# A second-layer chain moved one step ahead, weights split in four and dummy matmuls in the opening

## The chip, the cores and the metric

The kernel runs on one core of one Trainium2 chip. The metric is the device time of one execution in microseconds (us), the median of several runs. The engines are named as in the profile: PE is TensorE (matmuls; PEld its weight loads), DVE VectorE, ACT ScalarE, POOL GpSimd, SP SyncE (which here only issues DMAs and DMA transposes).

## The reference

`x` has 2048 tokens of 512 numbers in bf16. Four blocks follow one another, two layers of A and then B:

```python
def A(x, mem, Wq, Wk, Wv, Wo):            # 32 heads of 128
    for s in range(64):                   # segments of 32 tokens
        h = concat([mem, x[32*s:32*s+32]])       # 8 memory rows + 32 tokens
        q, k, v = h @ Wq, h @ Wk, h @ Wv         # per head
        p = softmax(mask(q @ k.T / sqrt(128)))   # memory is seen by all, tokens causally
        o = (p @ v) @ Wo
        mem, out[s] = o[:8], o[8:]               # the next segment needs mem
def B(x, wqkv, wo):                       # linear attention, 32 heads of 16
    q, k, v = x @ wqkv
    pq, pk = phi(q), phi(k)               # phi(t) = (t+1 if t > 0 else exp(t)) + 1e-6
    kv, z = pk.T @ v, sum(pk)             # over all 2048 tokens
    return (pq @ kv) / (pq @ z + 1e-6) @ wo
x = x + A(LN(x)); x = x + B(LN(x)); x = x + A(LN(x)); x = x + B(LN(x))
```

A is a recurrence: segment s+1 can't be finished before the 8 memory rows that segment s produces. B needs the sums over all tokens (`kv`, `z`) before any token's output.

## The kernel before

**Steps and tiles.** A segment is a *step* s, 0 to 63 in each layer. Four steps make a *tile* of 128 tokens, and there are 16 tiles. Since the memory rows take 8 of 40 rows, a step's main block `hT` has 8 memory rows and the first 24 tokens of the segment; the last 8 tokens of the four segments of a tile are gathered in one block of 32 rows, the *left* block (`hTL`). Keys, queries and values of a left block are made once a tile, for four steps ahead (`left_block`, places left0, left1 and leftv); they must be there when the tile's first step begins.

**What one step does**, in the loop of `a_layer`: keys and queries of the main block (`project`, matmuls at L2154 and, with weights already loaded, L2042; `turned` evicts them at L1919 on ACT or L1920 on DVE and transposes them on DVE at L2173), values; for the 8 memory rows the scores, exponentials, sums and products with the values in two halves (`mem_attention`), the output projection (`out_proj`, L2408, then L2419 on DVE), and the product L2436 that picks the next memory rows out of it (`next_mem`). This is the chain from step to step. Beside it run the token rows of the same segment (`x_attention`), whose result joins the output projection a step later; the residual (`residual`, whose rows go by DMA from `y_sb` to `dx_sb`, issued on POOL at L1936 and on SP); and the B block's share. Everything that is not the chain is *fill* for TensorE.

**The B block inside the steps.** When a tile of A is complete, `b_in` normalises it, multiplies it by `wqkv` (`rows_of`, L2582), makes phi of keys in the buffer `e_sb` and of queries in `eq_sb`, adds to kv and z (L2653, L2660), and writes x to the scratch `xs` and phi(q) to the scratch `pq` in memory. Between the layers `b_mid` makes the block's final matrices. In the second layer, `tokens` calls `b_out` for each tile before its steps: it loads the x rows from `xs` (POOL, L1936), loads the transposed phi(q) rows from `pq` into `e_sb` by a DMA transpose on SP (L2082), multiplies by the summed z (`md`, 16 matmuls at L2054), takes the reciprocal, multiplies by kv and wo, and adds to x. Then `prepare` normalises the tile (places prep), turns it by another DMA transpose, and fills `hT` and the left block; then left0, left1 and leftv follow. So the second layer's chain from memory rows to the next tile's left keys and queries is: place bo, place prep, places left0 and left1. `e_sb` and the rooms for layer norm rows and reciprocals (`xlnT`, `vB`, `rB_sb`) are single buffers that `b_in` and `b_out` share. In the first layer, left blocks are fed straight from the input, and the left keys and queries of tiles 0 to 2 are made in the opening by `first_left_blocks` (places sk and sq).

**What sets the order.** Every instruction group is a *node*, recorded by `_Prog.add` under a place (layer, step, name) and a running count. Each node has a time in nanoseconds in the table `PLACE` (L16 to L1547), with a letter a or v where it may run on ACT or DVE. `schedule` sorts all nodes by these times; that is the whole order on each engine, and the letter chooses the engine. The times are a planner's due times, not measured ones; only their order enters the program. `schedule` also hands out the eight PSUM banks in that order, `finalize` places semaphore waits, and `emit` writes each engine's stream in order, so an instruction that waits holds up all that is behind it on its engine. `P.count += n` skips counts so that the table's entries stay with their nodes.

**The opening.** On SP's queue, one behind the other, stand the loads of Wk, Wq, Wv (4 MB each), 16 pieces of Wo (256 KB each) and wqkv (1.5 MB). ACT issues the memory rows and x of tile 0, POOL x of tiles 1 and 2 among some 50 instructions that make constants (place setup). TensorE transposes the x rows, multiplies by Wk as soon as it is there (sk, then the keys of step 0), then by Wq (sq, queries), then by Wv, and step 0 follows. A function `spin` for dummy matmuls is there, but nothing calls it.

Of the kernel before, what the change touches and what calls it, by code (L numbers as in the profile page):

```python
# [16 lines left out]
    (0, -9, 'setup'): '2751 2752 1621 15060 15061 16711 17238 20254 20902 21335 26596 31128 31613 36233 37053 37678 40093 41399 42472 43512 44808 60645 14865 0 560 1120 2190 2750 3310 17835 18402 18743 18744 18748 18959 18960 19391 20038 20470 21117 21333 21981 22197 22628 24910 25947 26595 27242 27673 27674 27675 27892 27891 29832 31127 32422 35143 39577a 17834 18745v 0 32839 35503 35506 36229 36234 29400 18746 0 0 0 0 0 0 0 0 0 0 0 0 0 0 0 0 0 0 0 0 0 0 0 0 0 0 0 0 0 0 0 0 0 0 0 0 0 0 0 0 0 0 0 0 0 0 0 0 0 0 0 0 0 0 0 0 0 0 0 0 0 0 0 0 0 0 0 0 0 0 0 0 0 0 0 0 0 0 0 0 0 0 0 0 0 27889 27890',  # L17
    (0, -4, 'start'): '19607a',
    (0, -2, 'leftv'): '37698 39210 39672 40371 41400a 41831 42471 42962a 44807 44810',
    (0, -2, 'prep'): '14142 14864 15059 15391 15647 16712 18006v 18749a 19393a 20471v 17833v',  # L20
    (0, -2, 'prepl'): '13340 14063 16713 18747 22198 22843 25550a',
    (0, 0, 'kq0'): '19821 20469 20901 22411 29615 29831 31126 31611 22843a 35502 32197v 34321',
    (0, 0, 'kq1'): '20685 22627 23714 26377 27672 28320 30046 30262 28751a 36228 34684v 32840a 35139',
    (0, 0, 'lq'): '730981 734917 735345 736139 737902 739038 739581 745577',
    (0, 0, 'lx'): '725135',
    (0, 0, 'mem0'): '36230 36232 37051 37314 37677 39560 40092 44809 43119 44811',
    (0, 0, 'mem1'): '36231 36726 37679 37681 42962 43400 43719 44806 45734 46451',
    (0, 0, 'next'): '48918 48972 49238v',
    (0, 0, 'out'): '45447 45515 46452 46605 46882 47101 47370 47588 48015a 48443',
    (0, 0, 'ql'): '35504a 34436a',  # L30
    (0, 0, 'sk'): '19390 21116 22196 23282 23707v 24430',
    (0, 0, 'sq'): '29183 29399 30910 31773 32197a 32838',
    (0, 0, 'v'): '39211 40967 41398 41830 42470a 44812a',
    (0, 0, 'x'): '38130 38346 38692 39560 39576 41401 40094 42262 48015 43282 43341 46451 48409 50344a 57004v 45446 46824 47807 48297 51423a 50345v',
    (0, 0, 'xl'): '1620',
    (0, 1, 'kq0'): '49480 49911 50343 50775 51855v 52419 51639a 52056',
    (0, 1, 'kq1'): '52419 52419 52501 52717 51206 51422 51638 51854 53141a 53782 52934a 52717a 52992',
    (0, 1, 'lq'): '756403 760618 760834 761049 762164 763460 764413 769975',
    (0, 1, 'mem0'): '52933 53423 53994 53795 54262 55249 55828 55830 55827 56230',
    (0, 1, 'mem1'): '53994 54876 55248 55829 55831 56230 56623 57442 56840 57443',  # L40
    (0, 1, 'next'): '59643 59697 59962a',
    (0, 1, 'out'): '56622 57003 57221 57440 58377 58378 58379 58717 58970a 59168',
    (0, 1, 'ql'): '40264a 39209v',
    (0, 1, 'res'): '65669 65917',
    (0, 1, 'sk'): '18958 20037 21332 21980 24908a 25549',
    (0, 1, 'sq'): '26161 26593 27456 28967 33316a 33958',
    (0, 1, 'v'): '52991 53523 54263 54444 55085v 56275a',
    (0, 1, 'x'): '55899 56274 57221 57444 57581 58716 58036 58376 59643 58718 58719 58969 59850 62803v 70329a 58851 58910 59168 59961 60644a 61939a',
    (0, 2, 'kq0'): '60212 60643 61075 61507 63018v 63151 62587a 63020',
    (0, 2, 'kq1'): '62802 63017 63290 63507 61938 62154 62370 62586 64587a 64588 63019a 63289a 63717',  # L50
    (0, 2, 'leftv'): '40535 42262 43511 44806 45446a 46088 47102 47371a 53348 57441',
    (0, 2, 'lq'): '762163 762379 763027 763243 764661 765609 767779 770110',
    (0, 2, 'lx'): '730981',
    (0, 2, 'mem0'): '63449 64586 65177 64958 65549 65916 66408 66717 66931 67239',
    (0, 2, 'mem1'): '64958 65176 65548 65668 65918 66158 66930 67238 67867 67868',
    (0, 2, 'next'): '70328 70382 70962v',
    (0, 2, 'out'): '67869 67870 67907 68125 68344 68562 68780 68999 69606a 69853',
    (0, 2, 'prep'): '15988 16710 16904 17237 17493 17968 18401v 26594v 20255a 24909v 29184a',
    (0, 2, 'ql'): '54469v 58910v',
    (0, 2, 'res'): '73922 79787',  # L60
    (0, 2, 'sk'): '19174 20253 21548 23498 27457a 27893',
    (0, 2, 'sq'): '28104 30478 30694 32421 35141a 35865',
    (0, 2, 'v'): '63723 64155 64959 65670 65916a 66933v',
    (0, 2, 'x'): '66408 66932 67451 67866 68781 69470 69130 68999 70496 69605 69853 69853 70753 75955a 81212v 69853 70436 70495 70641 70961a 71496v',
    (0, 3, 'kq0'): '71496 71537 72185 72616 73265a 73923 73921a 74831',
    (0, 3, 'kq1'): '73048 73696 74552 74559 70963 71969 73911 74127 75207a 75956 74551a 74830a 75955',
    (0, 3, 'lq'): '735345 757243 757954 760402 761049 762743 765002 785076',
    (0, 3, 'mem0'): '75206 75265 75836 75637 76342 77046 77047 77387 77180 77582',
    (0, 3, 'mem1'): '76343 76344 76658 77180 77045 77386 77975 78306 78192 78668',
    (0, 3, 'next'): '81044 81098 81364v',  # L70
    (0, 3, 'out'): '77974 78355 78573 78988 79060 79784 79785 79786 80399a 80569',
    (0, 3, 'ql'): '70193v 73911a',
    (0, 3, 'res'): '81365 89404',
    (0, 3, 'sk'): '18742 19606 21764 23066 27894a 28105',
    (0, 3, 'sq'): '31612 34437 35140 35142 37052v 37314',
    (0, 3, 'v'): '73264 74775 75837 75957 76659v 77388a',
    (0, 3, 'x'): '77386 77673 78027 78573 78987 79783 79442 79923 81098 80569 81211 81270 81364 85987a 86151a 80398 81152 81441 81499 86277v 86751v',
    (0, 4, 'kq0'): '81611 82043 82474 83122 83986v 84485 84485a 85065',
    (0, 4, 'kq1'): '82906 84486 84850 84851 83554 83769 83985 84485 85497a 85914 84904a 84849a 85332',
    (0, 4, 'lq'): '767175 767779 768593 774744 778783 779388 780112 785508',  # L80
    (0, 4, 'lx'): '754821',
    (0, 4, 'mem0'): '85496 85986 86358 87108 87110 87762 88094 88805 88311 88806',
    (0, 4, 'mem1'): '86518 86576 87327 87109 88311 88474 89023 89841 89022 90059',
    (0, 4, 'next'): '92261 92315 92581v',
    (0, 4, 'out'): '89403 89621 89840 90058 90276 90495 90713 90931 91358a 91786',
    (0, 4, 'ql'): '83987a 84848v',
    (0, 4, 'res'): '95415 97436 87107 87326 87544 87874 88092 88585 88804 89185 90495a 90713 92827 92824 95198 94120 92826 96826 94983 95199 97493',
    (0, 4, 'sk'): '25730 27241 27888 28536 30695v 30911',
    (0, 4, 'sq'): '32205 36835 37051 37680 38693v 38846',
    (0, 4, 'v'): '85064 85914 86151 86751 87763v 88093a',  # L90
    (0, 4, 'x'): '88585 91150 92825 92828 92829 94984 94119 94550 95414 96708 96825 97316 98357 99061a 100805v 96766 97375 97865 98804 102000a 104112a',
    (0, 4, 'xl'): '3810',
    (0, 5, 'kq0'): '92823 93254 93686 94118 95416a 96886 94982a 96885',
    (0, 5, 'kq1'): '94549 94765 94981 95197 95413 95628 95844 96060 96277a 97435 97434a 96484a 97866',
    (0, 5, 'lq'): '762595 763890 764412 765003 768386 771109 775937 776686',
    (0, 5, 'mem0'): '97433 97492 98359 97864 98708 100009 100144 100187 100143 100549',
    (0, 5, 'mem1'): '98277 98277 98911 98358 100008 101159 101478 101787 102002 102149',
    (0, 5, 'next'): '104710 104764 105030v',
    (0, 5, 'out'): '101014 101478 101489 102406 102543 102761 102979 103256 103683a 104111',
    (0, 5, 'ql'): '96827v 97437a',  # L100
    (0, 5, 'res'): '112945 107325',
    (0, 5, 'sk'): '25946 26809 27025 28751 30970a 31611',
    (0, 5, 'sq'): '32197 35505 37682 38130 39599a 40371',
    (0, 5, 'v'): '96276 96884 98360 99060 99400v 100550a',
    (0, 5, 'x'): '98468 99400 100008 100145 101012 101489 101607 102979 102405 102149 103198 103592 103710 110431a 105136v 103475 103534 103651 103822 105343v 105932a',
    (0, 6, 'bi'): '97867 98277 98471 98804 99060 101013 102001 104062 105031 111073 112515 114473 115695 118563 115731a 122891 139072 123323 141513 115356 115902 116404 124929',
    (0, 6, 'kq0'): '105465 106540 106544 107324 107832a 108473 107833v 108836',
# [1686 lines left out]
def _build_kernel(nc, A_x, A_mem0, A_Wq, A_Wk, A_Wv, A_Wo, A_seg_len, B_wqkv, B_wo, out):  # L1794
# [118 lines left out]
    P = _Prog(nc, banks)  # L1913
# [965 lines left out]
```

## Time and profile before

| | us |
|---|---|
| median of 3 runs (1577.38, 1580.69, 1579.38) | 1579.38 |
| the profiled execution | 1580.13 |
| its span (first to last instruction) | 1578.4 |
| mean granted TensorE clock | 0.997 |
| end of the opening: first product L2436 | 52.0 |
| first layer, steps 1 to 62 | 705.1 |
| joining of the layers (steps 63 and 0, `b_mid`) | 46 |
| second layer, steps 1 to 62 | 724.3 |
| tail behind them | 51 |

Landings in the opening, from issue to data: x of tile 1 at 8.6 us, of tile 0 at 10.1, of tile 2 at 10.2, Wk at 14.5, Wq at 25.7, Wv at 35.9, the last piece of Wo at 47.7, wqkv at 51.6.

How to read it: the page's busy shares say which engine has least idle time; the chain that ended last says what the end of the span hung on; the timeline lists single groups with start, length, engine, line, operation, tiles and what released them; the windows view gives, for a stretch, its length and then for PE, PEld, DVE, ACT and POOL the busy time with the number of instructions, then the granted clock, the DMA share and GB/s. Lines are those of the code above. The code counts the layers from 0; the text below calls its layer 0 "layer 1" and its layer 1 "layer 2".

### The profile page before, as it was taken

To read this page: it belongs to the slowest core of one execution; us is meant where nothing else is said; L and a number is where in the kernel's file an instruction comes from. 1 tells how busy PE (TensorE), PEld (TensorE's weight loads), DVE (VectorE), ACT (ScalarE), POOL (GpSimd) and SP (SyncE) were. 2 spreads that over 40 slices of the span, in tenths; PEclk is the share of its full clock that TensorE was granted. 3 is DMA by queue.
4 is the path that set the end of the run, shared out by engine and by line. 5 is a ranking of instruction groups with operands and counts; after the bars stand their busy time and mean duration, and the time that the engine had idled before them with its cause. 6 is when DMAs were issued, how large, how long until landed. Compare 5 with 4: busy or idle time off the path is not lost.

```text
span 1578.4 us, 97381 instructions
## 1 busy us (share of the span) xinstructions
PE 1511.5 (96%) x48481; PEld 822.8 (52%) x40705; DVE 1223.1 (77%) x3536; ACT 987.4 (63%) x3043; POOL 197.2 (12%) x396
## 2 busy tenths in 40 slices
PE   5899999999999999999999999999999999999997
PEld 2445555555555555555545555555555455555554
DVE  4577878887777788777878787888877787777778
ACT  2566665656666666665666666666576666576665
POOL 2011110111111011111111110111101011110110
PEclk9999999999999999999999999999999999999999
DMA  9301010110000000101310111111101111001124
GB/s 381 104 20 20 17 33 20 27 24 23 21 18 16 22 24 24 24 17 30 62 32 17 26 25 20 25 29 21 31 10 27 27 27 23 23 20 20 34 42 134
DMA packets 84819, 60.69 MB, mean 38 GB/s; under 512 B 64121, under 2 KB 78777, under 8 KB 82873
## 3 DMA queue, kind: packets, MB, share of 16 engines
q1 hardware_dynamic: 71096, 37.58, 9.7%
q0 software_dynamic: 13152, 16.75, 3.9%
q8 instruction: 349, 5.72, 1.5%
q14 instruction: 62, 0.50, 0.1%
q10 hardware_dynamic: 160, 0.14, 0.0%
HBM read 25.57 MB, written 11.67 MB: 24 GB/s over the span
## 4 chain that ended last, share of the span: by engine, by line
PE 83%; DVE 8%; ACT 4%; DMA 3%; issue 1%; POOL 0%; SPq 0%; DVEq 0%
PE pb L2154 31%; PE pb L2042 21%; PE pb L2408 18%; PE pb L2054 8%; PE pb L2582 2%; ACT arena_sb L1919 2%; DMA Wq_sb<-in_A_Wq_dram 2%; PE pb L2270 1%; DMA dx_sb<-y_sb 1%; DVE arena_sb L1920 1%; PE pb L2347 1%; PE pb L2436 1%; DVE arena_sb L2173 1%; DVE y_sb L2419 1%; DVE st_sb L2092 1%
## 5 line engine op out<-in xcount | busy, mean ns | idle before, releaser
L1919 ACT ACTIVATE arena_sb<-pb 128x512 bf16<-128x512 f32 (+5 forms) x1180 | 530.8, 483 | 320.4 <-PE pb L2042 162.1
L1920 DVE CAST arena_sb<-pb 128x512 bf16<-128x512 f32 (+4 forms) x591 | 297.7, 512 | 93.7 <-PE pb L2042 51.1
L2154 PE MATMUL pb<-Wk_sb,arena_sb 128*32 128x512 bf16 x4192 | 364.4, 383 | 5.5 <-ACT arena_sb L1919 3.3
L2408 PE MATMUL pb<-Wo_sb,arena_sb 128*32 128x256 bf16 x10368 | 337.6, 273 | 4.4 <-DVE arena_sb L2318 2.1
L2173 DVE STREAM_TRANSPOSE arena_sb<-arena_sb 128x256 f32<-128x256 f32 x640 | 266.2, 432 | 48.7 <-ACT arena_sb L1919 41.2
L2054 PE MATMUL pb<-arena_sb 128*32 128x128 bf16 (+2 forms) x10800 | 277.0, 208 | 14.8 <-DVE arena_sb L1920 4.9
L2408 PEld LDWEIGHTS pb<-Wo_sb,arena_sb 128*32 128x32 bf16 x10368 | 258.1, 96 | 48.7 <-DVE arena_sb L2318 14.7
L1936 POOL DMA_DIRECT2D dx_sb<-y_sb x246 | 125.3, 513 | 1152.4 <-DVE y_sb L2419 627.0
L2054 PEld LDWEIGHTS pb<-arena_sb 128*32 128x32 bf16 x10800 | 190.1, 95 | 147.5 <-issue 33.3
L2154 PE MATMUL pb<-Wq_sb,arena_sb 128*32 128x512 bf16 x3088 | 259.5, 382 | 1.5 <-DMA Wq_sb<-in_A_Wq_dram 0.4
L2042 PE MATMUL pb<-Wv_sb,arena_sb 128*32 128x512 bf16 x2560 | 251.6, 378 | 0.1
L2154 PE MATMUL pb<-Wv_sb,arena_sb 128*32 128x512 bf16 x2560 | 251.5, 378 | 0.1
L2154 PEld LDWEIGHTS pb<-Wk_sb,arena_sb 128*32 128x32 bf16 x4192 | 112.9, 97 | 193.2 <-issue 102.6
L2042 PE MATMUL pb<-Wq_sb,arena_sb 128*32 128x512 bf16 x2032 | 199.3, 380 | 0.0
L2154 PEld LDWEIGHTS pb<-Wq_sb,arena_sb 128*32 128x32 bf16 x3088 | 83.8, 97 | 97.2 <-issue 44.4
L1919 ACT ACTIVATE outW_sb<-pb 64x256 f32<-64x256 f32 x142 | 53.6, 378 | 106.0 <-PE pb L2408 90.1
L2419 DVE TENSOR_TENSOR y_sb<-pb,outW_sb 64x256 bf16<-64x256 f32 x162 | 68.7, 424 | 50.1 <-ACT outW_sb L1919 45.4
L2358 DVE TENSOR_TENSOR arena_sb<-arena_sb,bo_sb 128x512 bf16<-128x512 bf16 x256 | 103.5, 416 | 2.4
L2318 DVE TENSOR_TENSOR arena_sb<-pb,arena_sb 128x128 bf16<-128x128 f32 x252 | 72.9, 290 | 36.3 <-ACT arena_sb L2306 12.2
L2154 PEld LDWEIGHTS pb<-Wv_sb,arena_sb 128*32 128x32 bf16 x2560 | 70.5, 95 | 53.6 <-issue 29.5
L2042 PE MATMUL pb<-Wk_sb,arena_sb 128*32 128x512 bf16 x928 | 92.5, 379 | 0.0
L2293 DVE TENSOR_TENSOR arena_sb<-arena_sb 128x256 bf16<-128x256 bf16 x252 | 70.2, 281 | 24.2 <-ACT arena_sb L2285 21.1
(122 smaller groups left out, 1804.9 us busy)
## 6 DMA issues: line engine op xcount, KB each, us to landing
Wk_sb<-in_A_Wk_dram SPq DMA_DIRECT2D x1, 4096.0 KB, 13.7
Wq_sb<-in_A_Wq_dram SPq DMA_DIRECT2D x1, 4096.0 KB, 24.4
Wv_sb<-in_A_Wv_dram SPq DMA_DIRECT2D x1, 4096.0 KB, 34.1
Wo_sb<-in_A_Wo_dram SPq DMA_DIRECT2D x16, 256.0 KB, 7.4
xs_scratch<-x_sb POOLq DMA_DIRECT2D x32, 128.0 KB, 2.7
pq_scratch<-arena_sb POOLq DMA_DIRECT2D x27, 128.0 KB, 2.5
x_sb<-xs_scratch POOLq DMA_DIRECT2D x16, 128.0 KB, 3.3
dx_sb<-y_sb SPq DMA_DIRECT2D x126, 12.0 KB
```

Source lines behind the costliest of these rows:

```text
L1919: return e.activation(o() if callable(o) else o, i() if callable(i) else i, ACTF.Copy)
L1920: return e.tensor_copy(o() if callable(o) else o, i() if callable(i) else i)
L1936: add(eng, lambda e: e.dma_start(o, i), 0.55 if eng == "pool" else 0.66, reads=reads, writes=writes, dsem="%s%d" % (kind, k), lat=lat + (0 ...
L2042: return pe.add_instruction(mybir.InstMatmult(name=nc.get_next_instruction_name(), engine=mybir.EngineType.PE, ins=[pe.lower_ap(x), pe.low ...
L2054: r = pe.matmul(o[q], w[:, q], x, start=start, stop=stop, skip_group_check=True, tile_position=(0, 32 * j))
L2154: r = pe.matmul(o, blk[:, c, :], w, start=(c == 0), stop=(c == 3), tile_position=(0, 32 * j))
L2173: add("dve", lambda v: v.transpose(dst, src(img[:, k, :].bitcast(F32))), 0.445, reads=[("img", k, h) for h in range(2)], writes=[dkey])
L2293: add("dve", lambda v: v.tensor_tensor(Pm[:, k, :].rearrange("p (a j x) -> p a j x", a=2, j=4), PQ[:, r2, b, 0:64].rearrange("p (a x) -> p ...
L2318: add("dve", lambda v: v.tensor_tensor(oTb[:, s % NO, 16 * b:16 * b + 16, 0:8].rearrange("p (i j) q -> p j i q", i=4), heads(pv.f32()[:, 0 ...
L2358: add("dve", lambda v, b=b: v.tensor_tensor(Pbx[:, :, b, :].rearrange("p j (k x) -> p j k x", k=4), px[:, b, :].rearrange("p (k x) -> p k ...
L2408: r = pe.matmul(tl.f32()[32 * j:32 * j + 32, 0:256], oT[:, 4 * hh + n, :], Wo_sb[:, 8 * n + hh, 256 * d:256 * d + 256], start=(hh == 0 and ...
L2419: add("dve", lambda e: e.tensor_tensor(y, tl.f32()[a, 0:256], outW[c, v, :], ALU.add), c_dve(256), reads=[("outW", w), "y0"], tiles=[tl], ...
```

## The change

Three things, all in one edit:

1. **wqkv in four pieces.** The single load at the end of SP's opening queue is gone. Four loads of 384 KB (one of the four 128-row parts each) are issued on SP after the next memory rows of steps 0 to 3 of the first layer (place ldqkv).
2. **Dummy matmuls in the opening.** `spin` is rewritten: n nodes, each of 3 groups of four 512-column matmuls on a tile of ones into a PSUM tile that nobody reads. Eight nodes stand ahead of the first left blocks (after x of tile 0 has landed), four between the left keys and the left queries. TensorE executes 144 matmuls more.
3. **A new table of places.** The constants of the setup are issued on POOL in one go, behind the x loads of tiles 2 and 1 (before, the x loads and constants were mixed). In the second layer the places bo, prep, left0 and left1 of the next tile stand about one step (11 to 13 us) earlier, and the nodes around them are reordered within the steps. Places of steps in the first layer change a little.

```diff
 PLACE = {
...
+    (0, -3, 'spin'): '12342 12989 13737 14384 15032 15679 16327 16974',
+    (0, -1, 'spin'): '23448 25391 26038 26902',
+    (0, 0, 'ldqkv'): '49487',
+    (0, 3, 'ldqkv'): '81613',
...
-    (1, 20, 'bo'): '1018786 1005620 1011726 1012993 1014251 1018784 1022710 1022926 1023142 1023357 1025686',
+    (1, 20, 'bo'): '986628 997753 998894 999595 1004218 1005546 1009067 1009714 1009930 1010146 1010901',
-    (1, 22, 'prep'): '1026116 1026607 1027961 1031504 1033605 1039898 1040761v 1050298a 1050852a 1041520a 1052663v',
+    (1, 22, 'prep'): '1011590 1014533 1016457 1021222 1021651 1022127 1027571v 1034423a 1040049v 1046447a 1057273a',
-    (1, 22, 'left0'): '1041527 1042071 1043269 1043941 1046399v 1047215 1048570a 1050851',
+    (1, 22, 'left0'): '1027800 1028611 1028929 1031671 1032311a 1033209 1036320v 1040417',
-    (1, 22, 'left1'): '1046120 1046548 1047274 1053490 1054762v 1056458 1058644a 1058821',
+    (1, 22, 'left1'): '1041669 1042203 1044378 1044988 1046016v 1046879 1048606a 1051154',
...
-    load(wqkv_sb[:, :, :], B_wqkv.rearrange("(c p) f -> p c f", p=128), "wqkv", 51.5)
+    P.count += 1
...
-    SPIN = {}
...
+    def spin(layer, step, name, n, after=(), reads=(), fresh=1):
...
+        for i in range(n):
+            tl = P.tile()
+
+            def mm(pe, tl=tl):
+                x = one_sb[:, 0:128].unsqueeze(1).to_broadcast([128, 4, 128])
+                for u in range(3):
+                    for j in range(4):
+                        o, q = tl.f32()[32 * j:32 * j + 32, 0:512], slice(32 * j, 32 * j + 32)
+                        if u < fresh:
+                            r = pe.matmul(o, one_sb[:, q], x, start=True, stop=True, skip_group_check=True, tile_position=(0, 32 * j))
+                        else:
+                            r = again(pe, o, one_sb[:, q], x, True, True, (0, 32 * j), True)
+                return r
+            nd = add("pe", mm, c_pe(3, 512), reads=["one"] + list(reads), tiles=[tl])
+            nd.order.update(after)
+            after = [nd]
+        return after
...
+            done = []
+            last = spin(0, -3, "spin", 8, reads=[("x", 0)], fresh=3)
             for W, key, move, nm in ((Wk_sb, "Wk", left_keys, "sk"), (Wq_sb, "Wq", left_queries, "sq")):
                 for G in range(3):
                     for b in range(2):
                         at(2 * G + b, nm)
+                        n0 = len(P.nodes)
                         move(G, b, project(hTL[lroom(G)], [("hTl", lroom(G))], (W, key, b, True))[0])
+                        pe = [n for n in P.nodes[n0:] if n.engs == ("pe",)]
+                        if G == 0:
+                            for n in pe:
+                                n.order.update(last)
+                            done += pe
+                if nm == "sk":
+                    last = spin(0, -1, "spin", 4, done)
...
+            if first and s < 4:
+                nd = P.nodes[-1]
+                at(s, "ldqkv")
+                add("sp", lambda e, s=s: e.dma_start(wqkv_sb[:, s, :], B_wqkv.rearrange("(c p) f -> p c f", p=128)[:, s, :]), 0.45,
+                    after=[nd], writes=["wqkv"], dsem="dqkv%d" % s, lat=4.0)
```

More of the change, by code (lines that the diff above doesn't have):

```diff
@@ L2055, in tiled @@
         return r
-    SPIN = {}
     LATE = {0: (8, 9, 10, 11, 12, 13, 6, 7, 4, 5), 1: (4, 5, 6, 7)}
-    def spin(layer, step, name, units, cols=512, fresh=0):
+    def spin(layer, step, name, n, after=(), reads=(), fresh=1):
         P.at(layer, step, name)
-        tl = P.tile()
-        def mm(pe):
-            x = one_sb[:, 0:128].unsqueeze(1).to_broadcast([128, cols // 128, 128])
-            for i in range(units):
-                for j in range(4):
-                    o, q = tl.f32()[32 * j:32 * j + 32, 0:cols], slice(32 * j, 32 * j + 32)
-                    if 4 * i + j < 4 + fresh:
-                        r = pe.matmul(o, one_sb[:, q], x, start=True, stop=True, skip_group_check=True, tile_position=(0, 32 * j))
-                    else:
-                        r = again(pe, o, one_sb[:, q], x, True, True, (0, 32 * j), True)
-            return r
-        before = [o for o in P.nodes[-40:] if o.engs == ("pe",)]
-        nd = add("pe", mm, units * (cols / 2.4 + 3.0) * 1e-3, reads=["one"], tiles=[tl])
-        nd.order.update(before)
-        return nd
+        for i in range(n):
[14 more added lines that the diff above has]
+        return after
     ln_no = [0]
```

3040 rows, old and new, of the table PLACE are left out of this document.

## Prediction

> **What bounds the kernel.** I read the page first: busy time by engine and the chain that ended last.
>
> ```profile
> PE 1511.5 (96%) x48481; PEld 822.8 (52%) x40705; DVE 1223.1 (77%) x3536; ACT 987.4 (63%) x3043; POOL 197.2 (12%) x396
> ...
> PE 83%; DVE 8%; ACT 4%; DMA 3%; issue 1%; POOL 0%; SPq 0%; DVEq 0%
> ```
>
> TensorE is busy 96% of the span and holds 83% of the last chain. But a 512-column matmul is written as 0.40 us while the next group of four starts 0.216 us later (below), so busy time hides pauses under about 0.2 us. I therefore went through the timeline from start to start: 512 columns every 0.216 us for four matmuls side by side, 256 every 0.109, 128 every 0.056. What lies between starts beyond this pace is a wait. Call the sum of the paces of a step its **work**; a step runs from one L2436 (the product that makes the next memory rows) to the next. In layer 2, steps 1 to 62 hold 684.0 us of work and take 724.3: 40.3 us of waits. In layer 1 they take 705.1.
>
> Next, the opening, in the timeline of TensorE.
>
> ```profile
> 43.06 0.40 PE L2154 MATMUL pb<-Wv_sb,arena_sb 128*32 128x512 bf16 x4
> 43.27 0.40 PE L2042 MATMUL pb<-Wv_sb,arena_sb 128*32 128x512 bf16 x4
> ...
> 49.61 0.39 PE L2054 MATMUL pb<-arena_sb 128*32 128x128 bf16 x13
> 52.01 0.24 PE L2054 MATMUL pb<-arena_sb 128*32 128x128 bf16 x3 [2.01 <-issue]
> 52.02 0.26 PE L2436 MATMUL pb<-selm_sb,y_sb 128*32 128x16 bf16 x8
> ```
>
> A node of 16 matmuls stops after 13 for 2.01 us with no releaser. Three starts of a run can't wait for data, so the instructions themselves were missing. On SyncE's queue, at that time, 1.5 MB of wqkv is still on its way (issued at 41.51, 10.0 us to landing).
>
> The stretches with the granted clock (third column from the right) show what this costs after it.
>
> ```profile
> 26.20:29.60 3.40, 3.40 (x36) 1.33 (x32) 1.45 (x3) 1.23 (x3) 0.00 (x0) 0.50 1.01 422
> 29.70:33.10 3.40, 3.40 (x72) 1.66 (x68) 1.59 (x4) 0.69 (x2) 0.00 (x0) 1.00 1.02 422
> 53.50:56.90 3.40, 3.40 (x36) 1.03 (x24) 1.37 (x3) 0.60 (x1) 0.00 (x0) 0.50 0.00 0
> ...
> 52.00:64.50 12.50, 11.09 (x303) 5.43 (x259) 7.51 (x24) 5.90 (x18) 0.00 (x0) 0.86 0.02 4
> 64.50:75.10 10.60, 9.82 (x304) 4.98 (x260) 7.21 (x20) 6.62 (x22) 0.52 (x1) 1.00 0.08 18
> ```
>
> After each sparse stretch of TensorE (22.9 to 25.8, 50.0 to 52.0) comes one stretch of 3.4 us at half clock: 36 matmuls instead of 72. The step after the stop takes 12.5 us, the next one, with as many matmuls, 10.6.
>
> Last, four steps of layer 2 in one tile, 17 to 20.
>
> ```profile
> 988.00:999.60 11.60, 10.77 (x336) 5.43 (x280) 8.89 (x26) 6.91 (x24) 1.08 (x2) 1.00 0.12 30
> 999.60:1011.80 12.20, 12.20 (x404) 5.96 (x316) 10.23 (x30) 6.98 (x21) 0.51 (x1) 1.00 0.10 17
> 1011.80:1023.30 11.50, 11.50 (x382) 6.68 (x314) 9.95 (x30) 7.81 (x24) 0.51 (x1) 1.00 0.19 18
> 1023.30:1035.30 12.00, 11.92 (x409) 7.54 (x348) 9.60 (x27) 9.09 (x27) 3.62 (x7) 1.00 0.11 30
> ```
>
> 336 matmuls take 11.6 us, 382 take 11.5: a step has a floor set by its own chain (keys, scores, values, out, next rows), and fill below the floor is free. Beyond it each matmul costs its pace.
>
> **Part 1, wqkv and the spins (opening).** Removed: the one wqkv load behind Wo; Wo's last piece lands at 47.7 in any case. Added: four loads of 384 KB, one a step, on SyncE behind the next rows of steps 0 to 3; at the 422 GB/s of the stretches above each is 0.9 us of transfers where the DMA share is 0.02 to 0.08, and the first reader is the B block of tile 0, five steps on: nothing. Each waits on SyncE for its step's rows, and the queue behind it is the row moves of that step, which wait for the same rows. The constants on GpSimd follow the two x loads instead of standing between them; x of tile 2, the last to land (10.24), is issued 2.3 us earlier. Start of the transposes: 13.2 before; I take 12.7.
>
> The spins stand in TensorE's queue ahead of real work: 12 nodes of 3 groups, 36 x 0.216 = 7.8 us. Ahead of the first L2436 stand 24.7 us of real work (96 groups of 512 columns, 20.7, and 4.0 of smaller ones). Waits: from 34.9 on, before had 3.5 (1.8 for the first scores); the order after has the same chain, 4.0. Half clock: before ran at half from 13.2 to 19.4 (starts 0.427 apart), with pauses between; with no pauses I take 4 us at half, 2.0 lost. Sum 12.7 + 7.8 + 24.7 + 4.0 + 2.0 = 51.2, against 52.0. The stop of 2.0 goes with its cover: transfers end at about 47. And the 3.4 us at half after it go, 1.7. **Opening: -0.8 - 1.7 = -2.5.** Bounds: with clock at once and half the waits, next rows come no earlier than Wo allows (47.7 + 1.6): -4.4; with 6.8 us at half, the stop and the dip as before: 51.2 + 1.4 + 2.0 - 52.0 = +2.6.
>
> Here a page speaks against me. The Trainium skill, "Runtime: NRT & Kernel Launch", Instruction fetch mechanics, holds that instructions come in 16 KiB blocks fetched ahead, and the cost of crossing a block is "mostly hidden". The row of 2.01 us disagrees. By that rule the stop would not be a late block, and moving wqkv would not remove it: the third rival below.
>
> **Part 2, layer 2 one step ahead.** Nothing is added. In the order of instructions, rows from memory (b_out), layer norm, and left0/left1 of the next tile move: left0 (four nodes, 3.5 us with left1) from steps 2 mod 4 into steps 1 mod 4, b_out's five nodes (1.2) from 0 into 3. Mean work of the steps 0, 1, 2, 3 mod 4 goes from 11.0, 9.9, 12.1, 11.0 to 10.7, 11.0, 11.5, 10.9. The sum stays 684.0. Sorting the 62 steps by work, with the mean wait of each class in before:
>
> under 9.3: 1.99 us, 3 steps, after 2. 9.3 to 10: 1.73, 9 and 1. 10 to 10.6: 0.95, 7 and 8. 10.6 to 11: 0.54, 6 and 21. 11 to 11.3: 0.30, 14 and 11. 11.3 to 11.8: 0.47, 9 and 12. Above: 0.04, 14 and 7.
>
> The counts of before give back 40.3, those of after 33.9: **-6.4**. Bounds: a smooth curve (a parabola through the 62 points) gives -2.8; if every step came to 0.30, -21.7. I take the classes, the nearest rows; the low end is held by the chain's own floor.
>
> What moves with it: b_out's two loads. The x rows go into a slot freed a tile ago, behind the xs write on GpSimd. The transposed pq rows go into e_sb, which the B block of the tile before last reads until its kv and z matmuls. Between these and b_out's first matmul stand 10.5 us of TensorE work on average before, 5.5 after (4.0 to 9.3).
>
> ```profile
> L2082 SPq DMA_TRANSPOSE arena_sb<-pq_scratch x13: 1198/1199/2237, 870.6 to 1437.5; - x13
> ...
> DMA to landing us min/median/max: 2.8/3.6/4.2
> ```
>
> With what SyncE has ahead of it, from the end of the last read to landing it was 2.9 to 5.8 us, 4.2 on average, the long ones behind a row move of the same moment; after, that row move stands behind it, so 2.9 to 3.6. I cost it at nothing; cover 5.5 us.
>
> Layer 1 (its order within steps changes slightly, and the work of its steps 0 to 3 mod 4 stays at 11.0, 9.5, 10.6, 10.8) and the tail (the last 48 us, with the same 42.3 of work): nothing, give or take 1.5.
>
> **Sum.** -2.5 - 6.4 = -8.9. The profiled execution is 1580.13 (span 1578.4 and 1.7 around it): 1571.2. It lies 0.75 above the median of the three runs, 1579.38, so the forecast is **1570.5**. Its own range is 1566.5 to 1574.
>
> **Rivals.** (1) The evened steps don't pay: steps 1 mod 4 wait on DVE and ACT as before and left0 is added on top. For it: in layer 1, whose left blocks already stand apart, steps 1 mod 4 still take 11.4 for 9.5 of work. Then only the opening is left: 1576.9. Chance 0.11. (2) The step ahead isn't there to be had, tiles wait for b_in anyway: the order after does place left0 a step earlier in 12 of 13 tiles, so 0.03; also 1576.9. (3) The stop stays, as a mechanism of the queue: 256 more instructions of the spins move the place where instructions run out, it falls elsewhere under Wo's transfers, and the dip follows: opening +1.2 instead of -2.5, 1574.2. Chance 0.14. (4) **Slower**: the pq transpose lands late. Place: b_out's first matmul in TensorE's queue, 13 tiles. It decides from about 5.9 us after the last read of e_sb; at 6.4 us the shortfalls against the 13 covers (4.0, 5.8, 6.2, 4.1, 6.4, 5.7, 5.6, 4.4, 4.8, 4.5, 4.9, 6.0, 9.3) add up to 14.4, so 1584.9. Against: the longest before is 5.8. Chance 0.05.
>
> The forecast has 0.67. The range leaves out rival 4, half of 1 and 2, and the ends of the unknown opening and of the parabola: 1565.5 to 1577.0. About 0.2% (3.2 us) is what a measurement of this kernel can tell from no change. Faster by more: the forecast, rival 3, and little of rival 1, 0.84. Within: 0.11. Slower: 0.05.
>
> **What would show it.** Opening: first L2436 product at 50 to 52 us, no releaserless stop, granted clock 1.00 from 26 on. Layer 2: steps 1 mod 4 near 11.5 us with some 380 matmuls, steps 2 mod 4 under 12; waits of layer 2 near 34. Rival 4 shows as waits of L2054 on the transposed load. Wrong would be: layer 1 changed by more than 2 us, or steps 1 mod 4 above 12.

## The result

The changed kernel takes **1571.3 us** (median of 6 runs, 1570.9 to 1572.5), the kernel before beside it 1579.2 (6 runs, 1576.1 to 1581.9). The ratio is 0.9946, interval 0.9929 to 0.9963. The forecast was 1570.5.

The page of the changed kernel answers the two lines shown of before: busy times first, then the chain that ended last by engine.

```profile
PE 1512.1 (96%) x48625; PEld 819.2 (52%) x40817; DVE 1223.5 (78%) x3533; ACT 985.3 (63%) x3046; POOL 197.5 (13%) x396
...
PE 87%; DVE 6%; ACT 3%; DMA 2%; issue 1%; POOL 0%; SPq 0%; DVEq 0%; POOLq 0%
```

TensorE has 144 instructions more and stays at 96% of a shorter span (1569.2); its share of the last chain rises from 83 to 87%, those of DVE and DMA fall. Where the time went, by the start of the product for the next memory rows (L2436, now L2452), in the two profiled executions:

| stage | before | after | difference | forecast |
|---|---|---|---|---|
| start to the first product | 52.02 | 49.02 | -3.0 | -0.8 |
| step 1 | 12.47 | 10.69 | -1.8 | -1.7 |
| layer 1, steps 2 to 62 | 692.6 | 691.7 | -0.9 | 0 |
| joining (to step 0 of layer 2) | 46.0 | 46.2 | +0.2 | 0 |
| layer 2, steps 1 to 62 | 724.3 | 718.7 | -5.6 | -6.4 |
| tail | 51.0 | 52.9 | +1.9 | 0 |
| span | 1578.4 | 1569.2 | -9.2 | -8.9 |

**The opening's end**, in the timeline of TensorE after the change (start, length, engine, line, operation, tiles, and in brackets an idle time with what ended it):

```profile
48.55 0.39 PE L2048 MATMUL pb<-Wv_sb,arena_sb 128*32 128x512 bf16 x4
49.02 0.22 PE L2452 MATMUL pb<-selm_sb,y_sb 128*32 128x16 bf16 x8
49.57 0.40 PE L2160 MATMUL pb<-Wk_sb,arena_sb 128*32 128x512 bf16 x4 [0.33 <-DVE arena_sb L1926]
```

The stop of 2.01 us without a releaser is gone, and the half-clock stretch behind it too, as the windows show (after the length: busy time and instructions of PE, PEld, DVE, ACT, POOL; then granted clock, DMA share, GB/s):

```profile
26.20:29.60 3.40, 3.40 (x68) 1.44 (x48) 1.70 (x5) 1.48 (x3) 0.00 (x0) 1.00 1.01 419
...
49.00:59.70 10.70, 9.34 (x296) 4.98 (x252) 7.75 (x24) 5.69 (x18) 0.00 (x0) 1.00 0.16 41
59.70:70.40 10.70, 9.88 (x311) 5.04 (x270) 7.32 (x21) 6.62 (x22) 0.52 (x1) 1.00 0.20 54
```

The third column from the right is 1.00 in every row, and steps 1 and 2 now take the same time.

**Steps 17 to 20 of layer 2** after the change, the same four as shown of before:

```profile
981.00:994.50 13.50, 12.71 (x360) 5.59 (x280) 6.95 (x21) 7.90 (x27) 1.63 (x3) 1.00 0.15 36
994.50:1006.20 11.70, 11.38 (x399) 6.06 (x331) 9.96 (x31) 7.77 (x23) 0.91 (x2) 1.00 0.07 17
1006.20:1017.20 11.00, 11.00 (x364) 6.07 (x297) 9.75 (x29) 7.51 (x21) 0.68 (x2) 1.00 0.07 19
1017.20:1028.90 11.70, 11.38 (x395) 7.22 (x342) 10.02 (x28) 7.77 (x26) 0.51 (x1) 1.00 0.03 6
```

The work is spread as forecast, though steps 1 mod 4 hold 355 matmuls on average (340 before) and not 380. The time of the first row doesn't fit: 360 matmuls in 13.5 us, where 336 took 11.6 before. The mean of all steps 1 mod 4 went from 11.47 to 11.77 us (work 9.94 to 10.96), of steps 2 mod 4 from 12.18 to 11.80 (12.12 to 11.52), of steps 3 mod 4 from 11.47 to 11.21. By class, steps 1 mod 4 lost 4.8 us in all, steps 2 gained 6.1, steps 3 gained 3.9 and steps 0 gained 0.4. Step 17's reason is in the timeline of DVE:

```profile
981.81 0.29 DVE L2379 TENSOR_TENSOR arena_sb<-arena_sb 128x256 bf16<-128x256 bf16 x1
985.26 0.42 DVE L2501 TENSOR_TENSOR x_sb<-x_sb,dx_sb 128x512 bf16<-128x512 bf16 x1 [3.15 <-DMA dx_sb<-y_sb]
985.72 0.69 DVE L2098 BATCH_NORM_STATS2 st_sb<-x_sb 128x6 f32<-128x512 bf16 x1
986.44 0.18 DVE L2099 BATCH_NORM_AGGREGATE st_sb<-st_sb 128x2 f32<-128x6 f32 x1
986.54 0.74 DVE L2179 STREAM_TRANSPOSE arena_sb<-arena_sb 128x256 f32<-128x256 f32 x2
```

In steps 1 mod 4 the residual add (L2485, now L2501) waits for the row moves by DMA, here 3.15 us, and the key and query transposes of the step's chain are queued behind it. This wait lies in both kernels: DVE stood 10.3 us in 13 such waits before and 18.0 in 14 after, in one execution each. It is also where executions differ most. Over four executions of the new order 28 of the 62 steps of layer 2 agree within 0.05 us, but step 17 took 13.47 in this one and 12.3 to 12.4 in the other three, and step 37 took 12.15 in three and 13.93 in one.

**The transposed phi(q) rows** (rival 4): the view of that DMA in the same stretch as before, with those who waited for it (the engine, the line, us, times).

```profile
L2088 SPq DMA_TRANSPOSE arena_sb<-pq_scratch x13: 1195/1200/2282, 862.2 to 1426.6; - x13
...
  PEld pb L2060: 0.9, 1
  PE pb L2060: 0.3, 1
...
DMA to landing us min/median/max: 2.0/2.7/4.4
```

13 transposes held TensorE once, at 1005.88 us: the two lines are the idle times of weight load and matmul before that same moment, 0.9 and 0.3 us. The rival counted 14.4.

**The start of the opening.** TensorE began at 13.24 before and begins at 10.45 after:

```profile
10.45 0.62 PE L2115 MATMUL pb<-id_sb,arena_sb 128*32 128x128 bf16 x16 [10.45 <-DVE arena_sb L2104]
10.85 2.77 PE L2076 MATMUL pb<-one_sb 128*32 128x512 bf16 x24
```

What TensorE waits for begins on DVE with the first sums of a layer norm, which wait for an x load. Before, and then after:

```profile
10.26 0.69 DVE L2092 BATCH_NORM_STATS2 st_sb<-x_sb 128x6 f32<-128x512 bf16 x1 [10.26 <-DMA x_sb<-in_A_x_dram]
```

```profile
7.82 1.29 DVE L2098 BATCH_NORM_STATS2 st_sb<-x_sb 128x6 f32<-128x512 bf16 x2 [7.82 <-DMA x_sb<-in_A_x_dram]
```

In both kernels the first sums are those of tile 2, whose x was issued at 3.07 and landed at 10.24 before, and was issued at 1.33 and landed at 7.80 after. The second sums are those of tile 0. The new order of places also swaps ACT's two issues: x of tile 0 goes out at 0.80 instead of 1.43, ahead of the memory rows, and lands at 3.67 instead of 10.13. x of tile 0 alone doesn't move the start much (x0_first, below); had x of tile 2 alone come earlier, the second sums would still have waited until 10.13.

### The profile page after: what moved, and what is told of

Read it like the earlier page. It is cut to its first block, busy times and chain, and to the rows that moved or that the text cites. A ratio compares the mean times of both kernels' runs of the same rounds, so it can differ in the third digit from the quotient of the medians.

```text
span 1569.2 us, 97666 instructions
## 1 busy us (share of the span) xinstructions
PE 1512.1 (96%) x48625; PEld 819.2 (52%) x40817; DVE 1223.5 (78%) x3533; ACT 985.3 (63%) x3046; POOL 197.5 (13%) x396
## 4 chain that ended last, share of the span: by engine, by line
PE 87%; DVE 6%; ACT 3%; DMA 2%; issue 1%; POOL 0%; SPq 0%; DVEq 0%; POOLq 0%
PE pb L2160 32%; PE pb L2048 21%; PE pb L2424 18%; PE pb L2060 9%; PE pb L2603 2%; PE pb L2286 2%; DVE arena_sb L1926 1%; DMA dx_sb<-y_sb 1%; ACT arena_sb L1925 1%; PE pb L2363 1%; PE pb L2452 1%; DVE y_sb L2435 1%; ACT outW_sb L1925 1%; DMA arena_sb<-arena_sb 1%; PE pb L2294 1%
## 5 line engine op out<-in xcount | busy, mean ns | idle before, releaser
L1926 DVE CAST arena_sb<-pb 128x512 bf16<-128x512 f32 (+4 forms) x609 | 302.3, 507 | 89.0 <-PE pb L2048 51.3
L2060 PE MATMUL pb<-arena_sb 128*32 128x128 bf16 (+2 forms) x10800 | 269.5, 208 | 12.2 <-DVE arena_sb L1926 3.8
L2305 ACT ACTIVATE arena_sb<-pb 128x160 bf16<-128x160 f32 x256 | 77.8, 306 | 14.7 <-PE pb L2286 7.1
```

What stands on the lines that cost most here:

```text
L1926: return e.tensor_copy(o() if callable(o) else o, i() if callable(i) else i)
L2060: r = pe.matmul(o[q], w[:, q], x, start=start, stop=stop, skip_group_check=True, tile_position=(0, 32 * j))
L2305: add("act", lambda a: a.activation(PQ[:, r2, b, 64:224], tl.f32()[:, 64:224], ACTF.Exp, scale=SCALE), c_act(160), tiles=[tl], writes=[("P ...
```

## Experiments

All ratios are to the kernel before on the same chip, with 95% intervals. In some an order is put together from two tables of places: the nodes up to a point in the order of one kernel, all others behind them in the order of the other.

### One half of the change at a time

**open_only**: the changed code; after's places up to the wqkv piece of step 3, before's from there on.

```diff
-    (1, 22, 'left0'): '1027800 1028611 1028929 1031671 1032311a 1033209 1036320v 1040417',
+    (1, 22, 'left0'): '1041527 1042071 1043269 1043941 1046399v 1047215 1048570a 1050851',
...
```

> The changed opening (spins, wqkv in four pieces, constants after the x loads, new order up to the next rows of step 3), then the order of before to the end. Theory (the terms add up, each in its own stage): first L2436 product at 49.0 us as in the changed kernel, step 1 without a half-clock stretch, so -4.8 us against before by step 2, all of it kept to the end: ratio 0.9970. Rival (the opening's gain is given back where steps wait for something not on TensorE's queue, a DMA or the joining of the layers): less than half is left at the end, ratio 0.9985 or more.

Measured 1576.0 against 1579.2, 0.9982 (0.9971 to 0.9993). The profiled execution had its first product at 50.46 (a half-clock stretch at 37.8 us and a stop of 0.56), step 1 at 10.93: -3.1 by step 2, and a layer 1 that was 1.8 us longer (five stops of over 0.3 us inside groups of matmuls, 3.7 us, against three with 1.7 in before). So by the times the opening is worth -2.8 (-4.6 to -1.1), not -4.8. The theory's 0.9970 lies just below the interval and the rival's 0.9985 inside it; that later steps give part of the gain back is not excluded.

**layer2_only**: before's code, before's places up to the next rows of step 62 of layer 1, after's from there on.

```diff
-    (1, 20, 'bo'): '1018786 1005620 1011726 1012993 1014251 1018784 1022710 1022926 1023142 1023357 1025686',
+    (1, 20, 'bo'): '986628 997753 998894 999595 1004218 1005546 1009067 1009714 1009930 1010146 1010901',
...
```

> The opening and the first layer of before, from the next rows of its step 62 on the order of the changed kernel. Theory (evened steps): layer 2's steps 1 to 62 take 718 to 719 us instead of 724.3; with the tail 1.9 longer, as in the changed kernel's profile, -3.7 us, ratio 0.9977; -5.6 and 0.9965 if the longer tail was chance. Rival (the two profiled executions differ by chance in layer 2): 723 to 725 us there, ratio 1.000 or more.

1573.0 against 1579.2, 0.9953 (0.9935 to 0.9970): -7.4 (-10.3 to -4.7). Layer 2 took 720.35 us, with step 37 at 13.93. Over the executions profiled here, the old order of layer 2 took 724.3, 725.3, 724.8, 725.1 (before, open_only, wqkv_four, x0_first), the new one 718.7, 720.4, 719.5, 719.2 (after, layer2_only, no_spins, wqkv_back): **-5.5 us**, and no overlap. The tail took 50.5 here. Over the executions it is 49.8 to 52.3 us in seven of the old order and 50.5 to 52.9 in four of the new one (means 50.9 and 51.6), so the longer tail of the profiled changed execution can't be told from chance. The two halves add up to -10.2, more than the -7.9 of the whole; their intervals allow for that.

### The opening, taken apart

**wqkv_four**: before, only wqkv moved.

```diff
-    load(wqkv_sb[:, :, :], B_wqkv.rearrange("(c p) f -> p c f", p=128), "wqkv", 51.5)
+    P.count += 1
...
+            if first and s < 4:
+                nd = P.nodes[-1]
+                at(s, "ldqkv")
...
```

> Before, with wqkv alone in four pieces behind the next rows of steps 0 to 3; no spins, order of before. Theory (late instructions behind wqkv's transfers): the stop of 2.0 us ahead of the first L2436 product goes, that product is at 50.0, and the half-clock stretch in step 1 goes too: -3.7 us, ratio 0.9977. Rival (the stop belongs to the place in the instruction stream, or to Wo's transfers): the stop stays, within 0.5 us of before, ratio 1.000.

1573.8, 0.9965 (0.9953 to 0.9978). First product at 50.19, step 1 at 10.69, so -3.6 there against before's profile. Where 13 matmuls were followed by 2.01 us of nothing, the timeline has all 16 in one piece:

```profile
49.55 0.51 PE L2058 MATMUL pb<-arena_sb 128*32 128x128 bf16 x16
50.19 0.22 PE L2440 MATMUL pb<-selm_sb,y_sb 128*32 128x16 bf16 x8
```

**wqkv_back**: the changed kernel with that load behind Wo again.

```diff
-    P.count += 1
+    load(wqkv_sb[:, :, :], B_wqkv.rearrange("(c p) f -> p c f", p=128), "wqkv", 51.5)
...
```

> The changed kernel with wqkv loaded in one piece behind Wo again, spins and order kept. Theory (instructions fetched late while 1.5 MB stand ahead of them): a stop of 1 to 2 us without a releaser comes back between 45 and 52 us, in some executions with a half-clock stretch behind it: +1 to +4 us against the changed kernel, ratio to before 0.9955 to 0.997. Rival (with the 144 added matmuls the edges of the instruction blocks lie elsewhere, and the wqkv load costs nothing there): ratio 0.9946.

1574.2, 0.9963 (0.9948 to 0.9978), 2.9 us above the changed kernel by the medians; the two intervals overlap, and the rival's 0.9946 lies just outside this one. The stop is back, inside a group of four, at another instruction than in before, and half clock behind it:

```profile
48.40 0.39 PE L2160 MATMUL pb<-Wv_sb,arena_sb 128*32 128x512 bf16 x3
51.16 0.39 PE L2160 MATMUL pb<-Wv_sb,arena_sb 128*32 128x512 bf16 x1 [2.37 <-issue]
```

```profile
52.30:55.70 3.40, 3.40 (x36) 0.85 (x20) 0.27 (x1) 0.77 (x2) 0.00 (x0) 0.50 0.02 5
```

One load in or out of the queue, in either kernel, takes or brings this stop: the cause is shown. All eight executions profiled with the load behind Wo have the stop, at least 1.15 us from start to start beyond the pace; of the six without it, four have none there and two a smaller one (0.6 and 0.4 us). The size differs between executions with one opening order: 2.2 us in three, 1.15 in three others (without a half-clock stretch behind it).

That the instructions were late is visible in the packets of the instruction queue (q8 in the profile's list of DMA queues, 16 KiB each). With before's opening, the packet ahead of the stop started at 49.4 to 49.5 us where the stop was 2.2 us long, at 48.1 to 48.6 where it was 1.15, and at 47.5 in wqkv_four, which has no stop. These packets took 1.0 to 1.2 us, and TensorE went on 1.3 to 1.4 us behind their end.

**x0_first**: before, ACT issues x of tile 0 ahead of the memory rows.

```diff
-    (0, -9, 'setup'): '2751 2752 1621 ...
+    (0, -9, 'setup'): '2753 2752 1621 ...
```

> Before, with one thing changed: ACT issues x of tile 0 ahead of the memory rows. Theory: x of tile 0 lands near 3.7 us instead of 10.1, the first transposes on TensorE start 1 to 3 us earlier, but without spins that time is lost again in the wait for Wq (25.7): first L2436 product within 0.5 us of 52.0, ratio 1.000. Rival (the start carries through to the end of the opening): first L2436 product at 49 to 50, ratio 0.9985.

1578.2, 0.9996 (0.9983 to 1.0009). x landed at 4.1 instead of 10.1, but DVE still waits for x of tile 2 until 9.96, and the first transposes start at 12.73, only 0.5 us earlier. The first product came at 50.78, 1.2 us earlier, with the stop (2.15) and a half-clock stretch still there. Neither expectation had the first product there, and the interval holds both ratios.

**no_spins**: the changed kernel without the dummy matmuls.

```diff
-        for i in range(n):
+        for i in range(0):
```

> The changed kernel without its 12 nodes of dummy matmuls; all else as changed. Theory (the loads set the opening's end: Wq 25.8, Wv 35.9, the last of Wo 47.2; the spins only keep the clock up): the first transposes stay at 10.5, TensorE pauses before Wk and before Wq and runs at half clock for 3.4 us after each, but the first L2436 product is within 1 us of 49.0: ratio to before 0.9946 to 0.9955. Rival (the spins carry the opening): first L2436 product at 51 to 52, ratio 0.996 to 0.9965.

1569.9, 0.9942 (0.9923 to 0.9961). First product at 49.42, step 1 at 10.73, as the theory had it; the 7.8 us of spins are worth nothing that can be measured. Without them TensorE sits idle 3.48 us before Wk and 0.19 before Wq. It begins the first scores at 34.10 instead of 36.94, then runs at half clock until 40.5. The first half of that stretch is short of work, the second is not: it holds 44 matmuls, and the changed kernel, at full clock, 88 in the same time. Head start and slower clock come out within 0.4 us of each other.

```profile
33.60:37.00 3.40, 2.50 (x44) 0.83 (x40) 3.26 (x8) 0.96 (x5) 0.00 (x0) 0.50 1.07 351
37.00:40.40 3.40, 3.40 (x44) 0.90 (x20) 0.05 (x1) 0.76 (x3) 0.00 (x0) 0.50 1.11 350
```

### Is fill below the floor free?

**fill_1mod4** and **fill_2mod4** add three groups of dummy matmuls per step to before, each a node of its own with a PSUM tile that nobody reads. The edit of the first (the second has `s % 4 == 2`):

```diff
+            if not first and s % 4 == 1 and 0 < s < 63:
+                for n in range(3):
+                    dummy(s, n)
```

> Before, with three groups of dummy matmuls (0.65 us of TensorE work) added to each of the 16 steps 1 mod 4 of layer 2, ahead of the second half of the first values product, of the output projection and of the next-rows product; 10.4 us of work in all. Theory (a step has a floor, and fill below it is free): by the waits of the classes of work, +0.6 us for all 16, ratio 1.0004. Rival (work adds up wherever it stands, the waits stay): +10.4, ratio 1.0066.

> The same three groups in each of the 16 steps 2 mod 4 of layer 2, which are full. Theory (floor): by the classes +9.8 us, ratio 1.0062. Rival (TensorE isn't the bound there, its pauses hide in busy time): +3 or less, ratio 1.002.

1589.0, 1.0069 (1.0052 to 1.0086), and 1591.9, 1.0087 (1.0070 to 1.0105). The second is as forecast and a little more; the first isn't: +10 where +0.6 was expected. Steps 1 mod 4 went from 11.47 to 12.05, 0.58 for 0.65 of work. **The floor as I had put it falls.**

**fill_own_tile**: the same groups, written into the tile of the matmuls behind them, at the places where before's trace has its longest pauses.

```diff
+            if P.place[2] == "out":
+                dummy(tl, 2, P.place[1])
...
```

> Before, with the same three groups of dummy matmuls in each of the 16 steps 1 mod 4 of layer 2 (10.4 us of work), but written into the PSUM tile of the real matmuls that follow, so that no bank more is needed, and placed where the trace of before has waits: ahead of the first key products, of the first values product, of the output projection. Theory (a pause of TensorE takes fill up to its own length for nothing; in the first trial the extra banks cost the rest): the pauses at these three places hold 6.4 us, each counted up to 0.216, so +4.0 us, ratio 1.0025. Rival (fill adds up in these steps too): +10, ratio 1.0065.

1584.9, 1.0053 (1.0037 to 1.0069): between the two. Layer 2 took 733.5, 9.2 more than before. Part of that is a new cost, in the waits of TensorE in layer 2 (who waited, for what, us, times, longest):

```profile
PE pb L2478 <- issue: 1.9, 6, 0.6
PE pb L2102 <- issue: 0.2, 1, 0.2
```

The output projection (there L2478) now stops six times in mid-group without a releaser; before's view of the same stretch has one such line of 0.5. From start to start there are 8 such stops of over 0.3 us in layer 2, with 3.6 us, against 1 with 0.7. An estimate, if each stop costs its length: 6.3 of the 10.4 us of fill were paid and 4.1 were free, where the pauses promised 6.4. (Layer 2 of fill_1mod4 took 13.5 us more than before and had 12 such stops with 6.7 us, so there 7.5 of 10.4 were paid.) By this estimate a pause of TensorE takes fill for about two thirds of its length.

### The wait for the row moves

**res_late_after** and **res_late_before**: in steps 1 mod 4 the residual add and the layer norm behind it stand behind the key and query transposes. Of the changed kernel's tile 3 in layer 1:

```diff
 place (0, 12, 'res'), node 20, and (0, 14, 'bi'), nodes 0 to 4
-187821; 188276 188999 189197 189529 189804
+190509; 190510 190511 190512 190513 190514
```

> The changed kernel with one thing moved: in the 24 steps 1 mod 4 of both layers where DVE's residual add (which waits for the row moves by DMA) and the layer norm behind it stand ahead of the key and query transposes, they stand behind them. Theory (the time by which steps 1 mod 4 vary from run to run, 11.4 to 13.9 us in layer 2, is DVE waiting for the row moves with the chain's transposes queued behind): those waits go, steps 1 mod 4 of layer 2 fall from 11.77 to about 11.4 on average and stop varying, -4 to -7 us in all, ratio to before 0.990 to 0.9925. Rival (the wait only moves to whoever needs the layer norm, the B block's products): within 2 us of the changed kernel, 0.9935 to 0.9955.

> The same move in the kernel before (25 steps). Theory (in before the wait lies in steps with 9.9 us of work, which have room for it, so less of it counts): -1 to -4 us, steps 1 mod 4 of layer 2 from 11.48 to about 11.3, ratio 0.9975 to 0.999. Rival (the row-move wait is all of the room in those steps, nothing else floors them): steps 1 mod 4 fall to near 10.5, -10 us or more, ratio 0.993.

1613.7, 1.0199 (1.0182 to 1.0216), and 1632.7, 1.0324 (1.0310 to 1.0338): **both theories wrong, by far**, and both rivals too. The wait did go (18.0 us in 14 waits in the changed kernel's profile, 1.0 in one here), and the chain paid for it at the next place, as DVE's timeline shows in step 17:

```profile
1021.10 0.38 DVE L2501 TENSOR_TENSOR x_sb<-x_sb,dx_sb 128x512 bf16<-128x512 bf16 x1
1021.51 0.69 DVE L2098 BATCH_NORM_STATS2 st_sb<-x_sb 128x6 f32<-128x512 bf16 x1
1022.24 0.18 DVE L2099 BATCH_NORM_AGGREGATE st_sb<-st_sb 128x2 f32<-128x6 f32 x1
1023.02 0.41 DVE L2104 TENSOR_SCALAR arena_sb<-x_sb,st_sb 128x512 bf16<-128x512 bf16 x1 [0.60 <-ACT st_sb L2102]
1023.35 0.28 DVE L2309 TENSOR_TENSOR arena_sb<-arena_sb 128x256 bf16<-128x256 bf16 x1
```

L2309 is the chain's product with the mask. 2.2 us of the B block stand ahead of it, 0.6 of them waiting for ACT. Steps 1 mod 4 went from 11.77 to 12.82 in layer 2 and, step 1 aside, from 11.31 to 13.03 in layer 1. The sparser TensorE also falls to half clock within the layers, 3.4 us each time: five times in res_late_after, twelve in res_late_before, never in the changed kernel or before.

**res_mid_after**: only 11 tiles, and the layer norm spread between the chain's operations (the add behind the transposes, the sums behind the two products with the mask, the last step 0.7 us later). Of tile 4 in layer 2:

```diff
 place (1, 16, 'res'), node 20, and (1, 18, 'bi'), nodes 0 to 4
-979771; 979772 980202 980418 980531 980559
+981897; 982390 982830 982831 982832 983529
```

> The changed kernel, in 11 tiles whose profile showed DVE waiting 0.8 us or more for the row moves: the residual add stands right behind the key and query transposes, the two sums of the layer norm behind the first and second product with the mask, its last step 0.7 us later. Theory (in the first trial 1.8 us of layer norm stood ahead of the chain's next DVE operation; spread like this they fit beside it): 0.3 to 0.5 us won in each of these steps, -3 to -5 us, ratio to before 0.9915 to 0.993. Rival (DVE has no room between the chain's operations in these steps): slower than the changed kernel, ratio 0.996 to 1.005.

1605.7, 1.0197 (1.0174 to 1.0219). The chain's waits were smaller, but the B block's own chain came late: its products (L2603) waited 1.2 to 2.9 us for the transposed rows in ten of the eleven tiles, and 0.7 in the other. Theory wrong again; the rival's direction is right, but the loss is larger than it said.

```profile
1345.07 1.26 PE L2424 MATMUL pb<-Wo_sb,arena_sb 128*32 128x256 bf16 x40
1348.71 0.62 PE L2603 MATMUL pb<-arena_sb 128*32 128x512 bf16 x4 [2.37 <-DMA arena_sb<-arena_sb]
```

In the changed kernel 4.3 to 5.1 us lie between the end of the layer norm and these products in nearly all tiles, and the DMA transpose between takes 3.2 (median). So steps 1 mod 4 carry a second chain: row moves, add, layer norm, DMA transpose, products. Both orders tried lose. Moving the products back with it was not tried.

## Why the prediction was right, and where it wasn't

- **Opening, -2.5.** Three executions with before's opening ended step 1 at 64.5 us, three with the smaller stop at 61.3 to 61.8, mean 63.0. Four with the changed opening (after, open_only, res_late_after, res_mid_after) have 59.7, 61.4, 61.2 and 59.6, mean 60.5. The difference is -2.6, and open_only's time gives -2.8. The two profiled kernels alone show -4.8, because before was caught with the longer stop and the changed kernel with none. Two of those four (open_only, res_late_after) also have a half-clock stretch at 37.8 us, which the forecast didn't have. The mechanism (late instructions behind wqkv, then half clock) is shown by wqkv_four and wqkv_back. Rival 3 is out: of its stop elsewhere, 0.6 and 0.4 us are left in two of six executions without the load.
- **That -2.5 fits so well is partly luck.** In the same means the first product moved by -1.7 and step 1 by -0.8, where the forecast had -0.8 and -1.7. The start was forecast 2.25 us too late; and the longer stop and the dip were counted whole, though half of the executions of before's opening have the smaller stop and no dip. The two errors nearly cancel.
- **The term that was mis-sized** is the start: "I take 12.7" for the transposes. It was 10.45. I looked at the right load: the earlier landing of x of tile 2 is 2.4 of the 2.8 us, and I counted 0.5. What I overlooked is x of tile 0 on ACT, which landed at 10.13 and would have been the next wait; the new order moved it as well. With 10.45 in the sum, 51.2 becomes 48.95; measured 49.02. Worked out from the trace of the changed kernel, from start to start, the other terms hold: work 24.6 us (24.7), spins 7.8, waits and half clock together 6.2 (6.0). What the sum doesn't show is that the spins cost nothing: without them waits and half clock come to 14.4.
- **Instruction blocks.** Behind the wqkv load the stops were 1.15 to 2.5 us in eight executions; without it, none in four and 0.6 and 0.4 in two. The Trainium skill ("Runtime: NRT & Kernel Launch", Instruction fetch mechanics) calls the cost of crossing a block "mostly hidden". The measurements decide: not beside this load. Nor does it take such a load. In seven traces 43 stops of over 0.5 us without a releaser stand behind step 1, up to 1.3 us long; each ended 1.2 to 1.6 us behind the end of an instruction packet, and in 15 of them no other transfer began in the 3 us before the stop or during it.
- **Layer 2, -6.4.** Measured -5.5; in the two profiles, waits 34.7 instead of 33.9. Steps 1 mod 4 came to 11.77 (forecast near 11.5, 12 was the limit), steps 2 mod 4 to 11.80. The size of the term was right; its reason, "fill below the floor is free", failed its own test. Dummy work set into these steps cost 10.0 of 10.4 us in the time (fill_1mod4, 0.6 expected) and 7.6 (fill_own_tile), while 1.02 us of left0 and reordered work cost 0.30 per step. So this term, too, owes part of its fit to luck. What shrank is visible by place, from start to start: the waits per step 1 mod 4 ahead of the first keys fell from 0.22 to 0.07 us, of the first values product from 0.25 to 0.07, of the second half's sums from 0.17 to 0.04. The new order does not only add fill there, it is arranged anew around the chain; that this is what made the added work cheap is argued, not shown.
- **Open**: how much of the -5.5 is left0's move and how much the new order within the steps. Putting most tiles' left blocks back alone was not tried. Open too is why wqkv_four gained as much as it did: its interval (-7.4 to -3.5) lies beyond the -2.2 that its end of step 1 (60.9) shows against the mean of 63.0, and open_only, which holds the same move, gained only 2.8.
- **Rival 1** (evened steps don't pay) is refuted by layer2_only, **rival 2** too; **rival 4** by the single wait shown above. In layer 1 and the tail no change can be told from chance: steps 3 to 62 of layer 1 took 680.1 to 683.7 us in eight executions of the old order and 681.1 to 682.8 in three of the new one.

## What to carry to other kernels

A stop inside a group of identical matmuls, with no releaser, was here the instruction stream running dry: see whether a packet of the instruction queue ends shortly before the stop does. If a bulk load is in flight beside it, move the load to where the DMA share is small. Two profiles are one draw each: where a term is a few us, collect it from every execution that shares the order in that stage. A forecast that comes out right in sum can be wrong in its parts: measure each part. A wait that stands in the middle of an engine's queue may hold a second chain's slack; before moving it, add up that chain to its end.

## What the runs showed of the hardware

- A load issued 0.63 us earlier landed 6.5 us earlier (x of tile 0: 0.80 to 3.67, against 1.43 to 10.13), beside 4 MB loads issued at 0.81 and 1.3 on SyncE. x of tile 2, issued 1.74 us earlier, landed 2.44 earlier.
- Adding 192 matmuls in layer 2 (fill_own_tile) brought stops without a releaser, also in steps where none were added (one of 0.7 us to eight with 3.6 in layer 2).
- A stop of TensorE without a releaser ended 1.2 to 1.6 us behind the end of a 16 KiB packet of the instruction queue, in the opening and in 43 stops behind it. Stops of 2.15 to 2.5 us in the opening had a half-clock stretch of 3.4 us behind them in five executions; stops of 1.15 us had none in three.
- Dummy matmuls that keep the clock up were worth nothing here: without them TensorE reached the first scores 2.8 us earlier, ran at half clock for 6.8 us, and had the first product 0.4 us later.
